# One step per chunk, crossbar transposes on the ACT queue and an earlier start of the weights, in a kernel that runs retention attention into an MLP

## The chip, the cores and the metric

The kernel runs on one core of one Trainium2 chip. The metric is the device time of one execution in microseconds (us). An execution more than 1.5% above the fastest of its kernel is counted as slow. "Median" is over four executions unless stated. A ratio is the mean time of one kernel's fast runs over that of the other's fast runs of the same rounds, so it is not quite the ratio of the medians quoted beside it; the brackets after it are a 95% interval. "Faster" or "slower" is given only where the difference is clearly over 2%.

Engine names: PE is the matrix engine, DVE the vector engine, ACT the scalar engine, POOL the general engine, SP the engine that here only starts transfers. "ACTq" and "SPq" in a timeline are DMA issues: the time an engine's instruction stream spends on starting a transfer.

## The reference

```python
# q, k, v: batch 8, heads 8, sequence 576, head size 64
scores = scale * q @ k.transpose
ret    = scores * D          # D[i, j] = gamma_h ** (i - j) for i >= j, else 0
x      = (ret @ v), heads side by side -> 4608 tokens x 512
h      = x @ w_in            # 512 -> 2048
g      = h * cos(h)
out    = g @ w_out           # 2048 -> 512
```

## The kernel before

Retention is computed in chunks of 128 tokens, five per batch entry, 40 in all (the fifth has 64 tokens). For each chunk PE does four things:

- scores: keys against queries, 64-row operands (row tiling), into PSUM `sc`; DVE masks it with a triangle into `pt`;
- state: keys against values, accumulated in PSUM `st`; DVE turns it into `sbd`, in which only each head's own block may be nonzero;
- inter: state of the chunk before times the queries;
- intra: `pt` times the values, 64-column outputs (column tiling); DVE multiplies inter + intra by the decay `up` and writes `xt`, the MLP's input.

The MLP then has units. An mlp1 unit is four matmuls into one PSUM bank, a sine on ACT (`cb`; the cosine is a sine with a shifted argument) and a product on DVE (`gt`), which frees the bank. An mlp2 unit is four matmuls; four units fill a bank that ACT copies to `os`. Chunks and units are interleaved in program order, and each engine works through its own instructions in that order.

Keys and queries are needed transposed. For the first seven chunks PE does it (`step_tk`, `step_tq`); later it is a crossbar DMA, issued from SP, which also issues the input loads and the output stores.

```python
def move_k(self, g):
    self.P.add("sp", lambda e: e.dma_start_transpose(KT[t] <- NAT[k]), ...)   # shortened
def move_q(self, d):
    self.P.add("sp", lambda e: e.dma_start_transpose(QT[t] <- QNAT[k]), ...)  # shortened
# ...
def step_st(self, g):
    def mm(e):
        for c in range(4):
            inst = e.matmul(
                ap(self.ST, 512, 0, 128, c * 128, [1, 128]),
                ap(self.NAT[k], 2 * DM, 0, n, c * 128, [1, 128]),
                ap(self.NAT[k], 2 * DM, 0, n, DM + c * 128, [1, 128]),
                start=(r == 0 and c == 0), stop=True, skip_group_check=True)
        return inst
    self.P.add("pe", mm, ...)
    self.P.add("dve", ... SBD = ST * BDM ...)     # 128x512 product with a block mask
# ...
BYPE, LEAD = 7, 2
def T(g):
    load_to(g + LEAD + 4)                # SP: loads
    cast_to(g + LEAD + 2)                # POOL: casts to bf16
    if g < BYPE:                         # PE transposes
        if pair(g):
            self.step_tq(dbl(g))
        self.step_tk(g)
    x = g + LEAD
    if BYPE <= x < NC:                   # crossbar transposes
        if pair(x):
            self.move_q(dbl(x))
        self.move_k(x)
# ...
def run(mlp, att):                       # spreads the attention steps over the mlp units
    n, m, k = len(att), len(mlp), 0
    for i, u in enumerate(mlp):
        u()
        while k < n * (i + 1) // m:
            att[k]()
            k += 1

def att_of(g0, g1):
    for g in range(g0, g1):
        out += [T(g + 1), ST(g), step_o(g), S_(g + 1)]    # as lambdas
```

The schedule has three stages. Stage 1 is the start-up and the first mlp1 pass. Stage 2 runs from the first mlp2 matmul to the first 512-wide mlp1 matmul after it; it holds the second block of mlp1 units (320 and 192 tokens wide) and about ten chunks. Stage 3 is the steady state, blocks of 512 tokens: 32 mlp units and about four chunks each, then a tail without chunks.

Of the kernel before, what the change touches and what calls it, by code (L numbers as in the profile page):

```python
# [101 lines left out]
class Kernel:  # L102
    def __init__(self, nc, es, q, k, v, w_in, w_out, out):
        self.nc = nc
        self.P = Prog(nc, es)
        self.src = [q.tensor, k.tensor, v.tensor]
        self.w_in, self.w_out, self.out = w_in.tensor, w_out.tensor, out.tensor
        sb = nc.alloc_sbuf_tensor
        self.NSTG, self.NNAT, self.NKT, self.NQ, self.NQT = 7, 6, 5, 3, 4
        self.NPT, self.NSB, self.NCB, self.NOS = 2, 2, 3, 3  # L110
        self.XT = sb("xt", [128, 4 * TOK], BF16)
        self.WIN = sb("win", [128, 4 * DFF], BF16)
        self.WOUT = sb("wout", [128, NF * DM], BF16)
        self.STG = [sb(f"stg{i}", [128, 2 * DM], F32) for i in range(self.NSTG)]
        self.NAT = [sb(f"nat{i}", [128, 2 * DM], BF16) for i in range(self.NNAT)]
        self.KT = [sb(f"kt{i}", [128, DM], BF16) for i in range(self.NKT)]
        self.QSTG = [sb(f"qstg{i}", [128, 2 * DM], F32) for i in range(self.NQ)]
        self.QNAT = [sb(f"qnat{i}", [128, 2 * DM], BF16) for i in range(self.NQ)]
        self.QT = [sb(f"qt{i}", [128, 2 * DM], BF16) for i in range(self.NQT)]
        self.PT = [sb(f"pt{i}", [128, 1024], BF16) for i in range(self.NPT)]  # L120
        self.SBD = [sb(f"sbd{i}", [128, 512], BF16) for i in range(self.NSB)]
        self.GT = [sb(f"gt{i}", [128, NF * TB], BF16) for i in range(2)]
        self.CB = [sb(f"cb{i}", [128, TB], BF16) for i in range(self.NCB)]
        self.OS = [sb(f"os{i}", [128, DM], F32) for i in range(self.NOS)]
        self.UP = sb("up", [128, 4 * S], F32)
        self.WV = sb("wv", [128, 40], F32)
        self.IDN = sb("idn", [128, 128], BF16)
        self.TRI = sb("tri", [128, 128], BF16)
        self.BDM = sb("bdm", [128, 128], BF16)
        self.ONE = sb("one", [128, 128], BF16)  # L130
        self.DUM = sb("dum", [128, 512], BF16)
        self.IG = sb("ig", [128, S], F32)
        self.IV = sb("iv", [128, 40], F32)
        self.LV = sb("lv", [128, 40], F32)
        self.LU = sb("lu", [128, 4], F32)
        self.CLN = sb("cln", [128, 1], F32)
        self.CPI = sb("cpi", [128, 1], F32)
        self.SC = nc.alloc_psum_tensor("sc", [128, 1024], F32)
        self.ST = nc.alloc_psum_tensor("st", [128, 512], F32)
        self.BK = [nc.alloc_psum_tensor(f"bk{i}", [128, 512], F32) for i in range(5)]  # L140
        self.held, self.turn = {0}, 0
        self.n_cb = self.n_os = 0
# [10 lines left out]
    def constants(self):  # L153
# [4 lines left out]
        P.add("pool", lambda e: e.iota(ap(self.IG, S, 0, 128, 512, [1, 64]), [[1, 2], [2, 32]], base=512,  # L158
                                       channel_multiplier=0, allow_small_or_imprecise_dtypes=True), w=["ig"])
# [3 lines left out]
        P.add("dve", lambda e: e.memset(self.DUM.ap(), 0.0), w=["dum"])  # L163
        for h in range(H):
            P.add("dve", lambda e, h=h: e.memset(ap(self.LV, 40, 0, 128, h, [8, 5]), -lng[h]), w=[("lv", h)])  # L165
            P.add("dve", lambda e, h=h: e.memset(ap(self.LU, 4, 64 * (h % 2), 64, h // 2, [1, 1]), lng[h]),
                  w=[("lu", h)])
        P.add("dve", lambda e: e.memset(self.CLN.ap(), math.log(1.0 / 8.0)), w=["cln"])
        P.add("dve", lambda e: e.memset(self.CPI.ap(), math.pi / 2), w=["cpi"])
        P.add("dve", lambda e: e.memset(self.BDM.ap(), 0.0), w=["bdm"])  # L170
        P.add("dve", lambda e: e.memset(ap(self.BDM, 128, 0, 64, 0, [1, 64]), 1.0), w=["bdm"])
        P.add("dve", lambda e: e.memset(ap(self.BDM, 128, 64, 64, 64, [1, 64]), 1.0), w=["bdm"])
        P.add("dve", lambda e: e.tensor_tensor(self.LV.ap(), self.IV.ap(), self.LV.ap(), ALU.mult),
              r=["iv"] + [("lv", h) for h in range(H)], w=["lvx"])
        P.add("act", lambda e: e.activation(self.WV.ap(), self.LV.ap(), AF.Exp), r=["lvx"], w=["wv"])
        for c in range(4):
            P.add("act", lambda e, c=c: e.activation(
                ap(self.UP, 4 * S, 0, 128, c * S, [1, S]), self.IG.ap(), AF.Exp,
                bias=self.CLN.ap(), scale=ap(self.LU, 4, 0, 128, c, [1, 1])),
                r=["ig0", "ig", "cln", ("lu", 2 * c), ("lu", 2 * c + 1)], w=["up"])  # L180
# [5 lines left out]
                                                channel_multiplier=-1), r=["one"], w=["tri"])  # L186

# [17 lines left out]
    def load_win(self, s, gate=()):  # L205
        self.P.add("pool", lambda e: e.dma_start(  # L206
            ap(self.WIN, 4 * DFF, 0, 128, s * 512, [DFF, 4], [1, 512]),
            bass.AP(self.w_in, s * 512, [[DFF, 128], [128 * DFF, 4], [1, 512]])),
            r=list(gate), w=[("win", s)], sem=f"wi{s}")
# [78 lines left out]
    def move_k(self, g):  # L288
        n, k, t = CHUNKS[g][2], g % self.NNAT, g % self.NKT
        self.P.add("sp", lambda e: e.dma_start_transpose(  # L290
# [3 lines left out]
    def move_q(self, d):  # L294
        n, k, t = (128, 128, 32)[d % 3], d % self.NQ, d % self.NQT
        self.P.add("sp", lambda e: e.dma_start_transpose(
# [11 lines left out]
    def step_s(self, g):  # L308
        n = CHUNKS[g][2]
        kt, pt, h = self.KT[g % self.NKT], self.PT[g % self.NPT], n // 2  # L310
# [10 lines left out]
        self.P.add("pe", mm, r=[("kt", g % self.NKT), self.qkey(g)], w=["sc"])  # L321
        self.P.add("dve", lambda e: e.tensor_tensor(  # L322
# [5 lines left out]
    def step_st(self, g):  # L328
        b, r, n = CHUNKS[g]
        k = g % self.NNAT  # L330

        def mm(e):
            for c in range(4):
                inst = e.matmul(  # L334
                    ap(self.ST, 512, 0, 128, c * 128, [1, 128]),
                    ap(self.NAT[k], 2 * DM, 0, n, c * 128, [1, 128]),
                    ap(self.NAT[k], 2 * DM, 0, n, DM + c * 128, [1, 128]),
                    start=(r == 0 and c == 0), stop=True, skip_group_check=True)
            return inst

        self.P.add("pe", mm, r=[("nat", k, 0), ("nat", k, 1)], w=["st"])
        self.P.add("dve", lambda e: e.tensor_tensor(  # L342
            ap(self.SBD[g % self.NSB], 512, 0, 128, 0, [128, 4], [1, 128]),
            ap(self.ST, 512, 0, 128, 0, [128, 4], [1, 128]),
            ap(self.BDM, 128, 0, 128, 0, [0, 4], [1, 128]), ALU.mult),
            r=["st", "bdm"], w=[("sbd", g % self.NSB)])

    def step_o(self, g):
        b, r, n = CHUNKS[g]
        na, pt, h = self.NAT[g % self.NNAT], self.PT[g % self.NPT], n // 2  # L350
        sbd = self.SBD[(g - 1) % self.NSB]
        i, ob, key = self.bank()

        def inter(e):
# [6 lines left out]
        def intra(e):  # L361
# [9 lines left out]
        if r:  # L371
            self.P.add("pe", inter, r=[("sbd", (g - 1) % self.NSB), self.qkey(g)], w=[key])
        self.P.add("pe", intra, r=[("nat", g % self.NNAT, 1), ("pt", g % self.NPT)], w=[key])
# [4 lines left out]
            r=[key, "up"], w=[("xt", g)])  # L378


    def mlp1(self, lo, hi, f):
# [17 lines left out]
        self.P.add("pe", mm, r=[("win", f // 4)] + xts, w=[key])  # L399
# [38 lines left out]
    def schedule(self):  # L438
# [4 lines left out]
        BYPE, LEAD = 7, 2  # L443
# [27 lines left out]
        def T(g):  # L471
            if g >= NC:
                return
            load_to(g + LEAD + 4)
            cast_to(g + LEAD + 2)
# [9 lines left out]

        def ST(g):
            if CHUNKS[g][1] < 4:
                self.step_st(g)

        def S_(g):  # L490
            if g < NC:
                self.step_s(g)
# [9 lines left out]
        def att_of(g0, g1):  # L502
            out = []
            for g in range(g0, g1):
                out += [lambda g=g: T(g + 1), lambda g=g: ST(g), lambda g=g: self.step_o(g), lambda g=g: S_(g + 1)]
# [14 lines left out]

        load_to(4)
        warm(10)
        for g in range(4):
            self.cast_k(g, "act")
            if g % 2 == 0:
                self.cast_q(g // 2, ("act", "dve"))
            self.cast_v(g, "pool")
            if g == 2:
                self.load_win(0, [("stg", 3, 0)])
                self.load_win(1)  # L530
            self.step_tk(g)
            if g % 2 == 0:
                self.step_tq(g // 2, "dve")
            if g:
                self.step_o(g - 1)
            self.step_s(g)
            self.step_st(g)
            if g < 3:
                warm(2)
        self.load_win(2)  # L540
        self.load_win(3)
# [4 lines left out]
        cast_to(6)  # L546
        self.mlp1(0, 256, 0)
        self.step_o(3)
        for f in (1, 2, 3):
            self.mlp1(0, 256, f)  # L550
# [6 lines left out]
        att = [lambda: T(4), lambda: S_(4)] + att_of(4, 7)  # L557
# [53 lines left out]
```

## Time and profile before

The median was 342.63 us (341.87 to 343.41, four runs).

| | start of stage 2 | start of stage 3 | span | stage 2 | stage 3 |
|---|---|---|---|---|---|
| before, profiled run, us | 35.9 | 96.1 | 339.4 | 60.2 | 243.3 |

From the page of the kernel before: the engines' busy times with share of the span and number of instructions, then three groups of instructions (line, engine, operation, output and inputs, shape, count; busy us, mean ns; idle us ahead of them and what ended most of it).

```profile
PE 311.9 (92%) x2184; PEld 158.8 (47%) x2220; DVE 189.8 (56%) x304; ACT 139.7 (41%) x223; POOL 96.3 (28%) x137
...
L393 PE MATMUL bk<-xt,win 128*128 128x512 bf16 (+3 forms) x640 | 147.5, 360 | 3.0 <-issue 1.3
...
L315 PE MATMUL sc<-qt,kt 64*128 64x128 bf16 (+1 forms) x320 | 16.1, 223 | 11.8 <-DMA kt<-nat 10.6
...
L334 PE MATMUL st<-nat 128*128 128x128 bf16 x128 | 13.5, 233 | 0.0
```

PE is the bottleneck on average. The one large idle term is scores (L315) waiting for transposed keys. ACT is busy 41% of the span. The PE timeline of the kernel before shows where the keys are late (start us, length us, what; in brackets the idle time before it and what ended it):

```profile
64.47 0.61 PE L315 MATMUL sc<-qt,kt 64*128 64x128 bf16 x8 [6.54 <-DMA kt<-nat]
```

Three more such waits, of 1.55, 1.88 and 0.66 us, follow by 96 us. The SP timeline of the same kernel shows what the keys stood behind:

```profile
58.96 2.89 SPq L296 DMA_TRANSPOSE qt<-qnat  x1
61.90 1.26 SPq L290 DMA_TRANSPOSE kt<-nat  x1
63.20 0.58 SPq L433 DMA_DIRECT2D out_dram<-os  x1
63.83 0.42 SPq L192 DMA_DIRECT2D stg<-in_k_dram  x1
```

The key transpose is issued only at 61.90, behind a query transpose that held SP for 2.89 us. In stage 3 there is no such wait, and the timeline of PE shows the shape of the work instead:

```profile
120.08 0.39 PE L356 MATMUL bk<-qt,sbd 128*128 128x128 bf16 x4
120.40 0.41 PE L364 MATMUL bk<-pt,nat 128*64 128x128 bf16 x8
120.75 1.04 PE L393 MATMUL bk<-xt,win 128*128 128x512 bf16 x4
121.62 1.03 PE L415 MATMUL bk<-wout,gt 128*128 128x512 bf16 x4
122.58 0.40 PE L315 MATMUL sc<-qt,kt 64*128 64x128 bf16 x8
```

Read the starts, not the lengths, because matmuls overlap: inter to intra is 0.32 us, intra to the next unit 0.35, and an mlp unit takes 0.87 from start to start. The state stands alone further up (119.00, and the next unit at 119.22). The four parts of a chunk sit in three places, with mlp units between them. The tiling mode of PE ("128*128", "64*128", "128*64") changes at intra and back, and at scores and back.

One block of 512 tokens took (262.42 - 129.84) / 4 = 33.1 us, from one block's first mlp1 to the same place four blocks on.

### The profile page before, as it was taken

What the parts mean: (1) busy time and instruction counts of PE and PEld (TensorE: products, weight loads), DVE (VectorE), ACT (ScalarE), POOL (GpSimd) and SP (SyncE); (2) the same over time, 40 slices, a digit from 0 to 9 for tenths busy, and PEclk for the clock granted to TensorE, in tenths of its full rate; (3) what the DMA queues carried; (4) which work ended last, traced back from release to release, by engine and by line L of the source; (5) the groups of instructions that cost most, each with busy time, mean ns of one, the idle gap of its engine ahead of it and who ended that gap; (6) DMA issues with size and microseconds to landing.
All of it is one profiled execution on the core that took longest, in us unless ns stands there. A gap on an engine that the chain in (4) does not pass through costs nothing.

```text
span 339.4 us, 5764 instructions
## 1 busy us (share of the span) xinstructions
PE 311.9 (92%) x2184; PEld 158.8 (47%) x2220; DVE 189.8 (56%) x304; ACT 139.7 (41%) x223; POOL 96.3 (28%) x137
## 2 busy tenths in 40 slices
PE   5799888498799999999999999999999999999997
PEld 2564344266554444444444444444444444444444
DVE  2697315288765766566665766566756565433300
ACT  7457332156333333334434334433343334444411
POOL 3460265545445443140424333322320000000000
PEclk9589999589899999999999999999999999999999
DMA  9999999999999997676669963847861101100012
GB/s 186 184 187 201 194 254 229 208 238 174 212 192 178 230 228 168 156 155 163 148 113 246 186 140 97 201 108 172 194 87 47 47 31 38 56 33 32 31 62 95
DMA packets 135307, 50.06 MB, mean 147 GB/s; under 512 B 108016, under 2 KB 130800, under 8 KB 135280
## 3 DMA queue, kind: packets, MB, share of 16 engines
q1 hardware_dynamic: 131056, 45.50, 63.9%
q0 software_dynamic: 4224, 4.19, 7.7%
q8 instruction: 18, 0.29, 0.4%
q14 instruction: 9, 0.07, 0.1%
HBM read 36.70 MB, written 9.44 MB: 136 GB/s over the span
## 4 chain that ended last, share of the span: by engine, by line
PE 70%; DMA 14%; SPq 6%; POOL 3%; issue 2%; DVE 2%; ACT 1%; DVEq 0%; POOLq 0%
PE bk L415 33%; PE bk L393 30%; DMA wout<-in_moe_w_out_dram 5%; DMA qstg<-in_q_dram 5%; DMA kt<-nat 4%; SPq L192 3%; PE sc L315 2%; PE bk L364 2%; DMA stg<-in_k_dram 2%; PE st L334 1%; PE bk L356 1%; POOL win L206 1%; DVE gt L403 1%; SPq L290 1%; SPq L200 1%
## 5 line engine op out<-in xcount | busy, mean ns | idle before, releaser
L400 ACT ACTIVATE cb<-bk,cpi 128x512 bf16<-128x512 f32 (+3 forms) x164 | 103.8, 635 | 151.3 <-PE bk L393 150.3
L403 DVE TENSOR_TENSOR gt<-bk,cb 128x512 bf16<-128x512 f32 (+3 forms) x164 | 101.8, 625 | 100.0 <-ACT cb L400 97.5
L393 PE MATMUL bk<-xt,win 128*128 128x512 bf16 (+3 forms) x640 | 147.5, 360 | 3.0 <-issue 1.3
L415 PE MATMUL bk<-wout,gt 128*128 128x512 bf16 (+1 forms) x573 | 142.1, 373 | 3.4 <-DMA wout<-in_moe_w_out_dram 1.3
L415 PEld LDWEIGHTS bk<-wout,gt 128*128 128x128 bf16 x592 | 55.3, 98 | 65.0 <-ACT os L430 3.7
L393 PEld LDWEIGHTS bk<-xt,win 128*128 128x128 bf16 x656 | 59.4, 100 | 54.7 <-DVE xt L374 2.1
L322 DVE TENSOR_TENSOR pt<-sc,tri 128x1024 bf16<-128x1024 f32 (+1 forms) x40 | 44.3, 1106 | 17.4 <-PE sc L315 17.4
L222 POOL CAST nat<-stg 128x512 bf16<-128x512 f32 (+1 forms) x36 | 21.9, 609 | 110.5 <-DMA stg<-in_k_dram 93.0
L232 POOL TENSOR_TENSOR nat<-stg,wv 128x512 bf16<-128x512 f32 (+1 forms) x40 | 41.7, 1043 | 24.2 <-DMA stg<-in_v_dram 15.1
L430 ACT ACTIVATE os<-bk 128x512 f32<-128x512 f32 (+1 forms) x37 | 21.7, 586 | 29.9 <-PE bk L415 29.9
L374 DVE TENSOR_TENSOR xt<-bk,up 128x512 bf16<-128x512 f32 (+1 forms) x40 | 26.7, 668 | 6.8 <-PE bk L364 6.7
L222 POOL CAST qnat<-qstg 128x512 bf16<-128x512 f32 (+1 forms) x44 | 25.8, 612 | 16.4 <-DMA qstg<-in_q_dram 15.4
L315 PE MATMUL sc<-qt,kt 64*128 64x128 bf16 (+1 forms) x320 | 16.1, 223 | 11.8 <-DMA kt<-nat 10.6
L342 DVE TENSOR_TENSOR sbd<-st,bdm 128x512 bf16<-128x512 f32 x32 | 21.8, 680 | 1.0 <-PE st L334 1.0
L315 PEld LDWEIGHTS sc<-qt,kt 64*128 64x128 bf16 (+1 forms) x320 | 9.3, 100 | 26.4 <-issue 12.7
L364 PE MATMUL bk<-pt,nat 128*64 128x128 bf16 (+1 forms) x320 | 16.2, 224 | 0.4 <-DVE pt L322 0.4
L334 PE MATMUL st<-nat 128*128 128x128 bf16 x128 | 13.5, 233 | 0.0
L334 PEld LDWEIGHTS st<-nat 128*128 128x128 bf16 x128 | 10.2, 104 | 6.4 <-issue 0.4
L356 PEld LDWEIGHTS bk<-qt,sbd 128*128 128x128 bf16 x128 | 9.7, 103 | 7.2 <-ACT cb L400 0.8
L364 PEld LDWEIGHTS bk<-pt,nat 128*64 128x64 bf16 (+1 forms) x320 | 10.0, 111 | 6.5 <-issue 2.5
L356 PE MATMUL bk<-qt,sbd 128*128 128x128 bf16 (+1 forms) x128 | 12.2, 221 | 0.6 <-DVE gt L403 0.6
L517 PE MATMUL bk<-dum,one 128*128 128x512 bf16 x15 | 6.8, 603 | 1.6 <-DVE lv L165 1.4
(36 smaller groups left out, 39.8 us busy)
## 6 DMA issues: line engine op xcount, KB each, us to landing
out_dram<-os SPq DMA_DIRECT2D x35, 256.0 KB, 2.2
stg<-in_k_dram SPq DMA_DIRECT2D x32, 256.0 KB, 3.6
qstg<-in_q_dram SPq DMA_DIRECT2D x16, 512.0 KB, 5.2
stg<-in_v_dram SPq DMA_DIRECT2D x32, 256.0 KB, 5.2
win<-in_moe_w_in_dram POOLq DMA_DIRECT2D x4, 512.0 KB, 8.3
wout<-in_moe_w_out_dram POOLq DMA_DIRECT2D x4, 512.0 KB, 14.9
stg<-in_k_dram SPq DMA_DIRECT2D x8, 128.0 KB, 3.3
qstg<-in_q_dram SPq DMA_DIRECT2D x8, 128.0 KB, 3.2
```

The costliest lines, as they stand in the source:

```text
L222: self.P.add(eng, lambda e: e.tensor_copy(dst, src), r=r, w=w)
L232: self.P.add(eng, lambda e: e.tensor_tensor(ap(self.NAT[na], 2 * DM, 0, n, DM, [D, H], [1, D]), ap(self.STG[st], 2 * DM, 0, n, DM, [D, H], ...
L315: inst = e.matmul(ap(self.SC, 1024, 0, n, hp * 512 + c * 128, [1, n]), ap(kt, DM, 64 * hp, 64, c * 128, [1, n]), self.queries(g, 64 * hp, ...
L322: self.P.add("dve", lambda e: e.tensor_tensor(ap(pt, 1024, 0, n, 0, [128, 8], [h, 2], [1, h]), ap(self.SC, 1024, 0, n, 0, [128, 8], [h, 2] ...
L334: inst = e.matmul(ap(self.ST, 512, 0, 128, c * 128, [1, 128]), ap(self.NAT[k], 2 * DM, 0, n, c * 128, [1, 128]), ap(self.NAT[k], 2 * DM, 0 ...
L356: inst = e.matmul(ap(ob, 512, 0, 128, c * 128, [1, n]), ap(sbd, 512, 0, 128, c * 128, [1, 128]), self.queries(g, 0, 128, c), start=(c == 0 ...
L364: inst = e.matmul(ap(ob, 512, 64 * hp, 64, c * 128, [1, n]), ap(na, 2 * DM, 0, n, DM + (2 * c + hp) * D, [1, D]), ap(pt, 1024, 0, n, hp * ...
L374: self.P.add("dve", lambda e: e.tensor_tensor(ap(self.XT, 4 * TOK, 0, 128, b * S + CH * r, [TOK, 4], [1, 2], [2, h]), ap(ob, 512, 0, 128, ...
L393: inst = e.matmul(ap(ps, 512, 0, 128, 0, [1, n]), ap(self.WIN, 4 * DFF, 0, 128, c * DFF + 128 * f, [1, 128]), ap(self.XT, 4 * TOK, 0, 128, ...
L400: self.P.add("act", lambda e: e.activation(ap(cb, TB, 0, 128, 0, [1, n]), ap(ps, 512, 0, 128, 0, [1, n]), AF.Sin, bias=self.CPI.ap(), scal ...
L403: self.P.add("dve", lambda e: e.tensor_tensor(ap(gt, NF * TB, 0, 128, f * TB + lo - TB * j, [1, n]), ap(ps, 512, 0, 128, 0, [1, n]), ap(cb ...
L415: return e.matmul(ap(ps, 512, 0, 128, 0, [1, cn]), ap(gt, NF * TB, 0, 128, f * TB + 128 * t, [1, 128]), ap(self.WOUT, NF * DM, 0, 128, f * ...
```

## The change

The intent has three parts.

1. One step per chunk: inter, state, intra and the next chunk's scores stand together, in an order with fewer changes of tiling mode. The state is computed only for each head's own 64 columns, so no mask is needed; two DVE copies of 64x256 replace the masked 128x512 product.
2. Crossbar transposes are issued from ACT instead of SP, and ahead of the loads in `T`; PE transposes now serve ten chunks instead of seven. The aim is that keys no longer wait behind loads and stores.
3. The start-up is reordered: w_in is issued sooner and its first pieces are smaller, the decay is computed in two parts.

```diff
 def move_k(self, g):
-    self.P.add("sp", lambda e: e.dma_start_transpose(
+    self.P.add("act", lambda e: e.dma_start_transpose(
 # ... and the same in move_q

+def mm_st(self, g):              # the state, 64 columns of one head at a time
     for c in range(4):
-        inst = e.matmul(ap(self.ST, 512, 0, 128, c * 128, [1, 128]), ...)
+        for hp in range(2):
+            inst = e.matmul(
+                ap(self.ST, 512, 64 * hp, 64, c * 64, [1, 64]),
+                ap(self.NAT[k], 2 * DM, 0, n, (2 * c + hp) * D, [1, D]),
+                ap(self.NAT[k], 2 * DM, 0, n, DM + (2 * c + hp) * D, [1, D]), ...)
+def ev_st(self, g):
-    # one DVE product 128x512 with the block mask
+    for hp in range(2):
+        self.P.add("dve", lambda e, hp=hp: e.tensor_copy(
+            ap(self.SBD[g % self.NSB], 512, 64 * hp, 64, 64 * hp, [128, 4], [1, 64]),
+            ap(self.ST, 512, 64 * hp, 64, 0, [64, 4], [1, 64])), ...)

+def step(self, g):
+    i, ob, key = self.bank()
+    self.mm_inter(g, ob, key)
+    self.mm_st(g)
+    self.mm_intra(g, ob, key)
+    self.mm_s(g + 1)             # the next chunk's scores
+    self.ev_o(g, ob, key)        # DVE: xt
+    self.ev_st(g)                # DVE: sbd, two copies
+    self.ev_s(g + 1)             # DVE: pt

-BYPE, LEAD = 7, 2
+BYPE, LEAD = 10, 2
 def T(g):
-    load_to(g + LEAD + 4)
-    cast_to(g + LEAD + 2)
     # ... the transposes ...
+    load_to(g + LEAD + 4)
+    cast_to(g + LEAD + 2)

-    out += [T(g + 1), ST(g), step_o(g), S_(g + 1)]
+    out += [T(g + 1), step(g)]

 # start-up, cut to what the argument touches
+    self.step_tk(1)
+    self.decay(256, S, "ig0", "ig1")     # second part of the decay, four Exp on ACT
+    self.sin_table()                     # makes ACT load the sine's table here
     # ...
+    self.load_win(0, 1, [("stg", 2, 0)]) # w_in one chunk sooner, in five loads for four, the first two half as large
     # ...
     self.cast_k(2, "act")
```

## The prediction

> **What bounds the kernel now.** Three stages, by the page's slices, the windows and the PE timeline.
> 1. 0 to 36 us: start-up, then the first mlp1 pass. The clock is 0.55 from 10 to 20 us; PE nearly gapless from 22.45 us.
> 2. 36 to 96 us: PE should do about 40 us of work (27.6 us of mlp, nine chunks, transposes) and takes 60. The PE timeline has gaps of 1.3, 1.3, 6.5, 1.6, 0.6, 1.9 and 0.7 us, the large ones ended by "DMA kt<-nat"; half clock follows two of them (about 4.5 us more). DMA moves 203 to 237 GB/s. The transposes sit on SP behind loads and stores; chunk 11's k load is issued at 63.8 us, behind two of them.
> 3. 96 to 323 us: PE-bound, 98% busy. One block of 512 tokens takes 33.1 us; its 32 mlp units are 27.65 us (0.864 each), so a chunk costs 1.25 us.
>
> **The change in stage 3.** Start to start, the timeline gives: state 0.22 us, inter 0.32, intra 0.35, scores 0.33 plus about 0.10 ahead of them. Streaming alone is about 0.21 each; the rest is switching. The Trainium skill (TensorEngine Tiling, Key Properties) says that changing the tiling mode drains the array, and this trace agrees, with about 0.1 us per change. One step per chunk (inter, state, intra, scores) has three changes for four and a state of half the columns: my estimate is 1.05 us for 1.25. 27 chunks: 5 us saved. DVE now gets 2.6 us in one burst after a step; the banks should cover it. A block's last step now stands just before the mlp1 that needs it: 0.2 us worse per block.
>
> **Crossbar transposes on ACT.** 30 kt and 18 qt issues, 1.25 us and 1.3 us (SP timeline, late, when unloaded; 2 to 3.7 us loaded), are about 61 us of ACT time (41% busy before). A pair blocks sin for about 2.6 us; banks allow about 3.5. Mostly hidden. The skill (DMA: Bandwidth & Descriptors, Issuing engines are not separate DMA queues) grants no bandwidth; the gain is order: loads no longer stand behind transposes, nor these behind stores.
>
> **Stage 2.** Chunks 7 to 9 now go through PE transposes, so the 6.5 us gap should vanish. But the first moved transpose (q10, ahead of the next sin) makes ACT wait for data that lands about 26 us after the weights: new PE gaps of 2 to 4 us there, and once or twice later. Estimate: stage 2 ends at 86 to 88 us instead of 96: 8 us saved.
>
> **Stage 1.** Weights start about 2.5 us sooner (the DMA gap at 15 to 18 us closes), removing the 1.3 us wait for wout. Scores 0 come 1.5 us sooner, but decay's second part and the sin table now precede chunk 2 on ACT. About zero on PE.
>
> **Sum:** 342.8 - 8 - 5 + 1 = 331 us, range 323 to 340. Chances: faster 0.74, same 0.19, slower 0.07.
>
> **Right if:** PE gaps at 57 to 96 us shrink from 11 to about 6 us; a block takes about 32.2 us; the state group falls from 13.5 to about 7 us busy; waits for kt nearly vanish; ACT waits on POOL casts appear near 57 us.
>
> **Wrong if:** transpose issues on ACT take 3 us each under load, sin comes late and PE waits for banks (DVE gt) throughout stage 3, eating the gain; or DMA, not order, limits stage 2 (chunk 15 no sooner than 89 us); or the half clock returns after a new gap.

## The result and the profile after

The median went up to 347.27 us (346.19 to 347.97, four runs), a ratio of 1.0132 [1.0097, 1.0168]: clear of noise, though under 2%. All outputs are right. The prediction was 331, with a range of 323 to 340: wrong in direction and outside the range.

| profiled run, us | start of stage 2 | start of stage 3 | span | stage 2 | stage 3 |
|---|---|---|---|---|---|
| before | 35.9 | 96.1 | 339.4 | 60.2 | 243.3 |
| after | 38.6 | 98.5 | 346.2 | 60.0 | 247.7 |
| difference | +2.6 | | +6.8 | -0.2 | +4.4 |
| predicted difference | 0 | | -12 | -8 | -4 |

(The spans are of one profiled run each; their difference of 6.8 us is larger than the 4.6 us between the medians, within the scatter of single runs.)

Against the prediction the shortfall is in every stage; against the kernel before, stages 1 and 3 are longer and stage 2 is as long as it was. From the page after: busy times, and the groups that answer to those shown of before.

```profile
PE 307.4 (89%) x2337; PEld 158.8 (46%) x2374; DVE 194.1 (56%) x335; ACT 141.6 (41%) x233; POOL 96.2 (28%) x138
...
L444 PE MATMUL bk<-xt,win 128*128 128x512 bf16 (+3 forms) x634 | 147.3, 363 | 21.0 <-DVE gt L454 8.0
...
L320 PE MATMUL sc<-qt,kt 64*128 64x128 bf16 (+1 forms) x320 | 15.9, 222 | 1.4 <-DVE qt L228 1.2
...
L346 PE MATMUL st<-nat 128*64 128x64 bf16 x256 | 10.4, 205 | 0.2 <-POOL nat L238 0.2
```

PE is busy 4.5 us less than before, which fits a cheaper step. The waits for keys are gone (11.8 us of idle ahead of scores became 1.4). But mlp1 (L444) now has 21.0 us of idle time ahead of it, where it had 3.0. ACT still reads "41%", because the issues it now makes are not counted. In the list of PE's waits (what waited, for what; total us, times, longest us) the kernel before had these:

```profile
PE sc L315 <- DMA kt<-nat: 10.6, 4, 6.5
PE bk L393 <- DVE xt L374: 1.3, 3, 0.6
PE bk L415 <- ACT os L430: 0.7, 1, 0.7
```

The list after names new ones:

```profile
PE bk L444 <- DVE gt L454: 8.0, 5, 2.6
PE bk L444 <- DVE xt L399: 7.5, 8, 1.8
PE bk L466 <- ACT os L481: 4.2, 4, 1.6
PE bk L266 <- ACT nat L226: 3.5, 2, 2.8
```

All four end in ACT or run through it, but not all of this is the transposes' doing: e1 below, without them on ACT, keeps part of it. **Stage 2**, the ACT timeline after, where keys of chunk 9 and the first moved transposes come:

```profile
61.96 0.59 ACT L226 ACTIVATE kt<-bk 128x512 bf16<-128x512 bf16 x1
63.21 1.33 ACTq L302 DMA_TRANSPOSE qt<-qnat  x1
64.57 1.69 ACTq L296 DMA_TRANSPOSE kt<-nat  x1
66.30 1.37 ACT L451 ACTIVATE cb<-bk,cpi 128x320 bf16<-128x320 f32 x3 [3.76 <-POOL nat L228]
```

The PE timeline after, just behind it:

```profile
67.57 1.25 PE L444 MATMUL bk<-xt,win 128*128 128x320 bf16 x8 [2.57 <-DVE gt L454]
```

The sine at 66.30 is said to have waited 3.76 us for POOL. Read the lines above it before believing that: ACT finished a copy at 62.55, waited 0.66 us for its data, and then spent 1.33 + 1.69 = 3.02 us on issuing two transposes. The few hundredths left are between the instructions. Then came the sine, then the product `gt` (66.93 in DVE's timeline), and only then did a PSUM bank come free for PE, which had stood still for 2.57 us.

**Stage 3**, the chain of waits after, around the place where a block of tokens ends (start us, length us, what):

```profile
130.33 0.69 ACT cb L451
131.02 0.56 ACTq L302
131.59 0.03 issue
131.62 1.69 ACTq L296
133.30 0.05 issue
133.35 0.70 ACT cb L451
...
134.14 0.69 DVE gt L454
134.83 0.64 DVE xt L399
135.47 0.27 issue
135.75 0.81 PE bk L444 x3
```

And the PE timeline of the same place:

```profile
132.72 0.39 PE L372 MATMUL bk<-qt,sbd 128*128 128x128 bf16 x4
133.04 0.32 PE L346 MATMUL st<-nat 128*64 128x64 bf16 x8
133.19 0.39 PE L387 MATMUL bk<-pt,nat 128*64 128x128 bf16 x8
133.51 0.40 PE L320 MATMUL sc<-qt,kt 64*128 64x128 bf16 x8
135.75 0.81 PE L444 MATMUL bk<-xt,win 128*128 128x512 bf16 x3 [1.84 <-DVE xt L399]
```

PE had finished intra by about 133.6, but `xt` started only at 134.75 in DVE's timeline (the chain counts it from the end of `gt`, 134.83). DVE works in order, and `gt` stood before `xt` in its stream; `gt` waited for the sine, and the sine for the two issues. The next block's first mlp1 needs this `xt`, and nothing is left between them to hide it. The waits for `os` arise on ACT alone, as its timeline and PE's show ten microseconds earlier:

```profile
122.28 1.19 ACTq L302 DMA_TRANSPOSE qt<-qnat  x1
123.51 1.27 ACTq L296 DMA_TRANSPOSE kt<-nat  x1
124.89 0.60 ACT L481 ACTIVATE os<-bk 128x512 f32<-128x512 f32 x1 [1.92 <-PE bk L444]
125.54 1.04 PE L466 MATMUL bk<-wout,gt 128*128 128x512 bf16 x4 [1.57 <-ACT os L481]
```

The copy to `os` stood behind the same two issues, and the next mlp2 unit behind the copy; the other long wait for `os`, 1.65 us at 260.76, looks the same.

**Stage 1**, the ACT timeline after:

```profile
10.12 2.28 ACT L185 ACTIVATE up<-ig,cln,lu 128x320 f32<-128x320 f32 x4
12.42 1.28 ACT L191 ACT_TABLE_LOAD   x1
13.82 0.61 ACT L226 ACTIVATE nat<-stg 128x512 bf16<-128x512 f32 x1
```

The keys of chunk 2 are cast at 13.82 (12.56 before), behind the second part of the decay and the table load. PE waited 2.80 us for that cast; before, PE waited for such a cast only once, 1.9 us, for chunk 0.

### The profile page after: what moved, and what is told of

Its sections match the earlier page's. It is cut to its first block, busy times and chain, and to the rows that moved or that the text cites. A ratio compares the mean times of both kernels' runs of the same rounds, so it can differ in the third digit from the quotient of the medians.

```text
span 346.2 us, 6065 instructions
## 1 busy us (share of the span) xinstructions
PE 307.4 (89%) x2337; PEld 158.8 (46%) x2374; DVE 194.1 (56%) x335; ACT 141.6 (41%) x233; POOL 96.2 (28%) x138
## 3 DMA queue, kind: packets, MB, share of 16 engines
q10 hardware_dynamic: 29184, 7.08, 13.1%
## 4 chain that ended last, share of the span: by engine, by line
PE 70%; ACT 6%; issue 6%; DVE 4%; POOL 4%; ACTq 3%; DMA 3%; SPq 3%; DVEq 0%; POOLq 0%
PE bk L444 33%; PE bk L466 29%; ACT cb L451 3%; ACTq L296 3%; SPq L198 2%; PE sc L320 2%; POOL nat L238 2%; DVE gt L454 2%; PE st L346 2%; DMA stg<-in_v_dram 2%; PE bk L387 2%; POOL qnat L228 2%; DVE xt L399 1%; PE bk L372 1%; DMA qstg<-in_q_dram 1%
## 5 line engine op out<-in xcount | busy, mean ns | idle before, releaser
L451 ACT ACTIVATE cb<-bk,cpi 128x512 bf16<-128x512 f32 (+3 forms) x164 | 102.6, 635 | 159.4 <-PE bk L444 119.7
L444 PE MATMUL bk<-xt,win 128*128 128x512 bf16 (+3 forms) x634 | 147.3, 363 | 21.0 <-DVE gt L454 8.0
L454 DVE TENSOR_TENSOR gt<-bk,cb 128x512 bf16<-128x512 f32 (+3 forms) x164 | 100.7, 624 | 108.8 <-ACT cb L451 87.0
L444 PEld LDWEIGHTS bk<-xt,win 128*128 128x128 bf16 x656 | 62.5, 101 | 80.7 <-DVE xt L399 9.4
L466 PEld LDWEIGHTS bk<-wout,gt 128*128 128x128 bf16 x592 | 56.1, 98 | 71.0 <-ACT os L481 9.0
L399 DVE TENSOR_TENSOR xt<-bk,up 128x512 bf16<-128x512 f32 (+1 forms) x40 | 26.7, 669 | 11.8 <-PE bk L387 10.9
L359 DVE CAST sbd<-st 64x256 bf16<-64x256 f32 x64 | 26.5, 414 | 1.0
L387 PEld LDWEIGHTS bk<-pt,nat 128*64 128x64 bf16 (+1 forms) x320 | 10.4, 114 | 1.6 <-DVE pt L331 1.1
L346 PE MATMUL st<-nat 128*64 128x64 bf16 x256 | 10.4, 205 | 0.2 <-POOL nat L238 0.2
L346 PEld LDWEIGHTS st<-nat 128*64 128x64 bf16 x256 | 6.8, 114 | 5.9 <-issue 3.5
L226 ACT ACTIVATE kt<-bk 128x512 bf16<-128x512 bf16 (+1 forms) x10 | 5.5, 550 | 4.6 <-PE bk L266 4.6
```

Source lines behind the costliest of these rows:

```text
L359: self.P.add("dve", lambda e, hp=hp: e.tensor_copy(ap(self.SBD[g % self.NSB], 512, 64 * hp, 64, 64 * hp, [128, 4], [1, 64]), ap(self.ST, 5 ...
L387: inst = e.matmul(ap(ob, 512, 64 * hp, 64, c * 128, [1, n]), ap(na, 2 * DM, 0, n, DM + (2 * c + hp) * D, [1, D]), ap(pt, 1024, 0, n, hp * ...
L399: self.P.add("dve", lambda e: e.tensor_tensor(ap(self.XT, 4 * TOK, 0, 128, b * S + CH * r, [TOK, 4], [1, 2], [2, h]), ap(ob, 512, 0, 128, ...
L444: inst = e.matmul(ap(ps, 512, 0, 128, 0, [1, n]), ap(self.WIN, 4 * DFF, 0, 128, c * DFF + 128 * f, [1, 128]), ap(self.XT, 4 * TOK, 0, 128, ...
L451: self.P.add("act", lambda e: e.activation(ap(cb, TB, 0, 128, 0, [1, n]), ap(ps, 512, 0, 128, 0, [1, n]), AF.Sin, bias=self.CPI.ap(), scal ...
L454: self.P.add("dve", lambda e: e.tensor_tensor(ap(gt, NF * TB, 0, 128, f * TB + lo - TB * j, [1, n]), ap(ps, 512, 0, 128, 0, [1, n]), ap(cb ...
```

## The experiments

The theory after reading the traces: the transposes cost the gain, through the 1.2 to 2.3 us during which each holds ACT's in-order stream; sine, `gt`, `xt` and `os` come late. Rivals: (a) the step itself, by its position just before the block that needs it, or by its burst of work on DVE; (b) the start-up's order on ACT; (c) data, not issue: ACT waits for the POOL casts that the transposes read, or the transfers themselves are slow; (d) ten PE-transposed chunks instead of seven. The first four runs shared one chip and one set of runs of the kernel before (median 342.32); then four (341.99), four (342.63) and two (342.26). Each of these groups ran on a chip of its own.

For stages 2 and 3 I made the same sums for each version: the listed waits of PE in the timeline, and the time lost to a halved clock, which is the length of a stretch times (1 - mean granted clock) from the windows view. The second counts idle time too, so it is a little high. All in us.

| version | stage 2 | PE waits | half clock | rest | stage 3 | PE waits | half clock | rest |
|---|---|---|---|---|---|---|---|---|
| before | 60.2 | 14.5 | 6.6 | 39.1 | 243.3 | 2.0 | 0 | 241.3 |
| after | 60.0 | 13.1 | 7.2 | 39.7 | 247.7 | 10.3 | 1.2 | 236.2 |
| e1 after, transposes on SP | 52.4 | 7.8 | 3.7 | 40.9 | 240.7 | 5.0 | 0 | 235.7 |
| e6 after, last step earlier | 56.9 | 12.1 | 4.0 | 40.8 | 239.7 | 0.7 | 2.7 | 236.3 |
| e5 e1, last step earlier | 51.0 | 8.3 | 1.5 | 41.2 | 237.0 | 0.7 | 0 | 236.3 |
| e8 e5, ACT order at start | 50.9 | 9.4 | 0 | 41.5 | 237.0 | 0.7 | 0 | 236.3 |
| e9 e1, seven PE chunks | 52.0 | 9.3 | 3.6 | 39.1 | 240.9 | 4.0 | 0 | 236.9 |
| e13 e9, loads first | 55.4 | 11.5 | 5.0 | 38.9 | 240.9 | 4.0 | 0 | 236.9 |

(Stage 2 waits include the one that ends where stage 3 starts. Stage 3 waits are summed from 100 us on, without gaps of 0.16 us that are put down to "issue": they come where a matmul's record is missing. The clock column of stage 3 is the half clock that still lasts at its beginning.) The "rest" columns hardly move. Stage 3 has about 236 us of work with the new step and 241 with the old one, whatever the queue; stage 2 has about 41 with ten chunks transposed on PE (after: 39.7) and 39 with seven. Nearly everything else is waits and the clock. Each row is one trace. After and e6 run the same program up to stage 3, and their stages 2 differ by 3.1 us (60.0 and 56.9), most of it the clock; e1 and e5, alike in the same way, differ by 1.4. So a difference of up to about 3 us in stage 2 between two rows proves nothing by itself.

### e1: the change, with the transposes back on SP

```diff
 # after; in move_k and move_q
-self.P.add("act", lambda e: e.dma_start_transpose(
+self.P.add("sp", lambda e: e.dma_start_transpose(
```

> The changed kernel with its crossbar transposes issued from SP again, in the same program order; nothing else differs. Theory A (the issues on ACT hold sin, os and then DVE behind them): the PE waits for xt at the block boundaries fall from about 0.96 us each to the 0.4 of before, the waits for os vanish, stage 3 shortens by 8 to 10 us, and the kernel takes 334 to 339 us. Rival B (the one-step order itself: its DVE burst and its place as the last unit of a block): the boundary waits stay at 0.7 us or more, and the time stays within 2 us of 347.

Measured: 333.15 us, ratio 0.974 [0.969, 0.979]. The queue of the transposes alone is worth 347.27 - 333.15 = 14.1 us; the two were run in different rounds, and by their ratios to their own before it is (1.0132 - 0.974) x 342.6 = 13.4 us. Stage 2 fell to 52.4, stage 3 to 240.7. Theory A is right about the time, but not in each of its numbers: stage 3 fell by 7.0 us and not by 8 to 10, stage 2 gave the rest, and the boundary waits stayed at 0.50 to 0.77 us, about what rival B said of them. The place in stage 3 that answers to the one shown of after, in the DVE timeline of this version:

```profile
124.33 0.69 DVE L454 TENSOR_TENSOR gt<-bk,cb 128x512 bf16<-128x512 f32 x1 [1.04 <-ACT cb L451]
125.11 0.73 DVE L399 TENSOR_TENSOR xt<-bk,up 128x512 bf16<-128x512 f32 x1
```

and in the PE timeline:

```profile
126.11 0.81 PE L444 MATMUL bk<-xt,win 128*128 128x512 bf16 x3 [0.72 <-DVE xt L399]
```

`gt` is on time: `xt` starts 0.91 us after inter (124.20 in PE's timeline) instead of 2.03 (132.72 to 134.75), and the mlp1 at 126.11 waits 0.72 us instead of 1.84. What remains, 0.72 us, is not the issues'; e5 shows that it belongs to the step's position.

Rival (c) can be read from the traces. In the ACT timeline of after, ACT stood idle ahead of only one of its 48 transposes, for 0.66 us (the one at 63.21 above); all others were issued while the instruction before them still ran or right behind it. So waiting for the casts cost ACT almost nothing, and the holes in its work are the issues. From issue to landing a key transpose took 3.9 us on the ACT queue and 3.2 on SP's (queries 5.2 and 4.5), so the transfer was slower from ACT, if anything, but PE waits for no crossbar keys in either. The mean issue time was 1.39 us for 30 key and 1.25 us for 18 query transposes on ACT, 64 us in total.

### e2: the kernel before, with the transposes on ACT

```diff
 # before; in move_k and move_q
-self.P.add("sp", lambda e: e.dma_start_transpose(
+self.P.add("act", lambda e: e.dma_start_transpose(
```

> The kernel before with only the issuing engine of the transposes changed, SP to ACT. Theory A: stage 3 gets longer by 6 to 10 us through late sin and os, time 348 to 354 us. Rival B: the position of the step is needed for the harm; stage 3 stays within 2 us of 217 us and the time within 3 us of 343.

Measured: 349.98 us, ratio 1.0228 [1.0164, 1.0292], so 7.7 us slower than before's 342.32. The move costs time without the rest of the change as well, so it is not an interaction with the new step alone. Its interval reaches across 2%. Stage 2 took 65.3 us for before's 60.2. In its list of waits stand 10.1 us for `gt` and 6.6 for `os` where before had 10.6 for keys and 0.7 for `os`: the wait was exchanged, not removed. The profiled run also had a stretch at 186 to 195 us with a mean clock of 0.62, which is worth 9 x 0.38 = 3.4 us of its stage 3 of 250.5; I do not use that stage's length. (The 217 us of the expectation is not stage 3 as defined here, which took 243.3 us before.)

### e3: the kernel before, with the new step alone

```diff
 # before, with after's mm_*, ev_* and step
-out += [T(g + 1), ST(g), step_o(g), S_(g + 1)]
+out += [T(g + 1), step(g)]
```

> The kernel before with only the one-step order and the 64-column state; transposes stay on SP, start-up and the seven chunks of PE transposes as before. Theory A: stage 3 shortens by 4 to 5 us, time 337 to 339 us. Rival B: boundary waits grow to about 1 us each and DVE bursts hold banks; time 343 us or more.

Measured: 341.37 us, ratio 0.997 [0.9931, 1.0009]: no difference that the runs resolve, and between the two expectations. In the stages, stage 3 gained 2.6 us (240.7 for 243.3) and stage 2 lost 1.7. The step does not cause the slowdown, but it also does not give its 5 us.

### e4: the kernel before, with the new start alone

```diff
 # before, with after's constants, decay, sin_table, load_win and start-up sequence
```

> The kernel before with only the start-up of the changed kernel: decay in two parts, sin table early, weights sooner and in finer pieces, other order of chunks 0 to 3. If the start-up is what lost time there: mlp2 begins 2.6 us later (38.5 instead of 35.9 us) and the time is 1 to 3 us longer, 344 to 346 us. If only the transposes did it: within 1 us of 343.

Measured: 340.07 us, ratio 0.9929 [0.9868, 0.9991]. Stage 2 started 2.1 us later (38.0) and was 2.6 us shorter; the weights' wait of 1.3 us is gone. The time met neither branch of the expectation: on balance the start is a small gain (the interval ends just under 1), so rival (b) is not what made the change slower. It could still be better than it is, which e7 tries.

### e5 and e6: the last step of a block earlier

In stage 3 the steps of a block are spread over all its 32 mlp units, so the last one stands right before the mlp1 that needs it. Here they are spread over the first 28. e5 is e1 with this edit; e6 is the changed kernel with it, transposes on ACT.

```diff
-def run(mlp, att):
-    n, m, k = len(att), len(mlp), 0
+def run(mlp, att, spare=0):
+    n, m, k = len(att), len(mlp) - spare, 0
     for i, u in enumerate(mlp):
         u()
-        while k < n * (i + 1) // m:
+        while k < min(n, n * (i + 1) // m):
 # the calls of stage 3:
-    run(mlp, att_of(need[j + 1], need[j + 2]) if j + 2 < NTB else [])
+    run(mlp, att_of(need[j + 1], need[j + 2]) if j + 2 < NTB else [], 4)
```

> The changed kernel with its transposes on SP, and the steps of a block spread over 28 of its 32 mlp units, so that the last step ends four units before the mlp1 that reads its xt. If the position of the last step costs what is left at the boundaries: the waits for xt, 6.2 us in all, fall to about 1 (those of stage 2 stay), and stage 3 falls from 240.7 to 236 to 237 us. If the waits come from the DVE burst wherever it stands: they move to gt or os, and stage 3 stays at 239 us or more.

> The changed kernel with its transposes still on ACT, and the steps spread over 28 of 32 units. If the ACT issues do their harm in stage 3 mainly through the boundary (late sin, late gt, late xt): stage 3 falls from 247.7 us to about 241. If they do it everywhere (os and banks), it stays at 244 us or more.

Measured: e5 329.10 us, ratio 0.9624 [0.9585, 0.9663]; e6 338.14 us, ratio 0.9893 [0.9851, 0.9934]. This pair decides stage 3. On SP the edit gained 3.7 us there (240.7 to 237.0), on ACT 8.0 (247.7 to 239.7). In e6 the PE timeline from 100 us on has no wait for `xt` at all and 0.7 us for `os`, where after had 5.8 and 4.5 us. With four units of slack, the same issues on ACT do no visible harm in stage 3: e6's stage is 2.6 us longer than e5's, and its first 14.2 us ran at a mean clock of 0.81 (e5: 1.00), which is 2.7 us carried over from stage 2. So in stage 3 the transposes on ACT hurt only with the steps spread to the block's end. For `xt` the reason is the missing slack; that the waits for `os` vanish too is measured, but not taken apart: the edit also moves the issues relative to the copies to `os`. In stage 2, e6 keeps most of the loss: 56.9 against 51.0.

### e7 and e8: the order on ACT at the start

e7 is e1 with the second part of the decay and the table load moved behind the casts of chunks 2 and 3; e8 is e5 with the same.

```diff
     self.step_tk(1)
-    self.decay(256, S, "ig0", "ig1")
-    self.sin_table()
     self.step_o(0)
     # ...
     self.cast_k(3, "act")
+    self.decay(256, S, "ig0", "ig1")
+    self.sin_table()
     self.cast_v(3, "pool")
```

> The changed kernel with its transposes on SP, and on ACT the second decay part and the sin table moved from before the casts of chunk 2 to after the cast of chunk 3's k. If that place delays the start: the 2.7 us PE wait for the cast of chunk 2's k vanishes, mlp2 begins 2 to 4 us sooner than the 38.5 to 40.6 us of the two runs that have it, and the time falls from 333 to 330 or 331 us, unless the data of chunk 4 then ends the wait. If not: within 1 us of 333.

> Both edits on top of the changed kernel with its transposes on SP. If the two gains add, since they lie in different stages: 326 to 329 us.

Measured: e7 330.67 us, ratio 0.969 [0.9644, 0.9735]; e8 327.06 us, ratio 0.9568 [0.9531, 0.9604]. Chunk 2 is cast at 10.59 us instead of 13.82, and PE's wait of 2.8 us for it is gone; part of it comes back as a wait for the cast of the next queries (2.4 us in e7, 1.5 in e1). Against e1 (another chip's rounds) e7's median is 2.5 us lower; against e5, of the same rounds, e8's is 2.0 us lower. Part of this is the clock: both ran stage 2 without any half clock, where e1 lost 3.7 us to it. The start of stage 2 is not a clean measure: after, e1 and e5 have the same start-up (no crossbar transpose is issued before 63 us in after), and reached stage 2 at 38.6, 40.6 and 38.4. From 20 to 30 us, after and e5 had a mean clock of 0.88 and 0.87, e1 0.71. The Trainium skill (TensorE: Matmul & The Clock Gate, What's actually happening) says that the activity window is free-running, so that one kernel's count of slow matmuls varies with its phase at the start. These three traces fit that, with 2.2 us between them; no run here isolates it.

### e9 and e13: seven chunks on PE, and the order of loads and transposes on SP

e9 is e1 with seven PE-transposed chunks as before; e13 is e9 with loads and casts ahead of the transposes again.

```diff
 # e9
-BYPE, LEAD = 10, 2
+BYPE, LEAD = 7, 2
 # e13, in T, in addition
+load_to(g + LEAD + 4)
+cast_to(g + LEAD + 2)
 # ... transposes ...
-load_to(g + LEAD + 4)
-cast_to(g + LEAD + 2)
```

> The changed kernel with its transposes on SP and chunks 7 to 9 back on the crossbar (seven chunks of PE transposes for ten). If the ten chunks are what closes the 6.5 us gap of stage 2: a PE wait of 6 us or more for kt comes back near 60 us, stage 2 falls back from 52.4 to 58 us or more, the time is 338 to 341 us. If the order of issue (transposes ahead of loads) closes it: no such wait, 333 us plus or minus 1.5.

> The changed kernel with transposes on SP, seven chunks of PE transposes, and, on SP and POOL, the loads and casts of later chunks ahead of the transposes again, as the kernel before had it. If the order transposes ahead of loads is what saved stage 2 (the previous run kept its 52 us without the three extra chunks): stage 2 goes back to 57 us or more with kt waits of 8 us or more, the time to 338 us or more. If neither the order nor the number of chunks matters by itself, and the sooner weights do it: stage 2 stays below 55 us.

Measured: e9 336.01 us, ratio 0.9798 [0.9732, 0.9864]; e13 338.36 us, ratio 0.9863 [0.9794, 0.9931]. With seven chunks the waits for keys come back (5.2 us in three waits in e9, 6.5 in two in e13), but stage 2 keeps its length (52.0 against 52.4), because waits for `gt` shrink and PE has fewer transposes to do (the rest falls from 40.9 to 39.1). Neither branch of e9's expectation was met. Ten against seven is therefore not settled: the medians of e1 and e9 differ by 2.9 us, across jobs, and the intervals of their ratios overlap. Issuing the transposes ahead of the loads on SP is worth about 3.4 us of stage 2 in the traces (55.4 against 52.0) and 2.4 us in the medians, again with overlapping intervals; 3.4 us is hardly more than the 3.1 by which two traces of one program differed. If it is real, it is the effect that the move to ACT was meant to have, and it was to be had on SP.

### e10 and e11: the order and the 64-column state apart

e10 is the kernel before in the one-step order, but with the 128-column state and the masked product. e11 is the kernel before in its old order, but with the 64-column state and the two copies.

```diff
 # e10: before with step(), mm_st as before (128 columns, BDM)
-out += [T(g + 1), ST(g), step_o(g), S_(g + 1)]
+out += [T(g + 1), step(g)]
 # e11: before with after's mm_st and ev_st, the old att_of
```

> The kernel before with the one-step order but the full 128-column state and its masked product. If a change of tile shape costs PE about 0.1 us: the state group stays 0.22 us long plus a change, one change per chunk is saved, 27 chunks give 2.7 us, and the later xt at six boundaries takes about 2.6 back, so stage 3 is 243 us plus or minus 0.7 and the time 342 to 344. If the order alone were the whole gain: stage 3 240.7 us as with both.

> The kernel before with the state in 64-column tiles but in the old order, the state alone between two mlp units. If a change of tile shape drains the array for 0.1 us: the state now has a change on each side that it had not, which is worth more than its halved columns, so stage 3 grows by 1 to 3 us, to 244.5 or 246 us. If halving the columns is a gain by itself: stage 3 falls by about 2.5 us.

Measured: e10 342.92 us, ratio 1.0004 [0.9957, 1.0051], stage 3 0.3 us shorter than before's: by the same sums the order saved 2.2 us of work there, and the late last step took 1.9 back in waits for `xt`. e11 344.99 us, ratio 1.0062 [1.002, 1.0104], stage 3 2.9 us longer. Together (e3) they were 2.6 us shorter, and with the last step early (e5) 6.3. Why the narrow state alone is worse is seen in the PE timeline of e11:

```profile
112.26 1.03 PE L459 MATMUL bk<-wout,gt 128*128 128x512 bf16 x4
113.22 0.32 PE L339 MATMUL st<-nat 128*64 128x64 bf16 x8
113.46 1.04 PE L437 MATMUL bk<-xt,win 128*128 128x512 bf16 x4
```

Between two mlp units it takes from 113.12 (112.26 + 0.86) to 113.46, 0.34 us, of which 0.10 is ahead of it; the 128-column state took 0.22, with the same tiling as its neighbours. The Trainium skill (TensorEngine Tiling (Array Packing), Key Properties) says that a change of tiling mode drains the array. The 0.10 us ahead of it and the 2.9 us of stage 3 fit that: the narrow tile pays only where it stands next to intra, which has the same mode. In the one step, state to intra is 0.15 us (133.04 to 133.19 above).

### e12 and e15: one of the two state copies on ACT

e8 with one copy of each pair on ACT, everywhere (e12) or in `step()` only (e15), to shorten DVE's burst after a step (`xt` 0.7, copies 0.86, `pt` 1.1 to 1.2 us).

```diff
 def step(self, g):
-    self.ev_st(g)                      # both copies on DVE
+    self.ev_st(g, ("dve", "act"))      # the second on ACT
```

> The fastest so far (transposes on SP, last step early, decay later on ACT), with one of the two copies of the state moved from DVE to ACT, so that DVE's burst after a step is 0.43 us shorter. If the burst is what holds banks in stage 2 (6.4 us of waits for gt): those fall to 4 or 5 us and the time to 325 or 326 us. If ACT is as tight there: 327 us or more.

> The fastest kernel so far with one of the two state copies on ACT in the steps only, not in the start-up, where the copy on ACT had made chunk 1's k wait. If the shorter DVE burst is worth the 3 us that stage 2 fell by (50.9 to 47.7 us), and the start-up is the 37.1 us of the kernel without it: 323 to 325 us. If the late start was chance (the clock) and stage 2 only took back what it lost: 326 to 328 us.

Measured: e12 327.67 us, ratio 0.9565 [0.952, 0.961]; e15 327.44 us (324.11 to 329.35), ratio 0.9523 [0.9454, 0.9592]. One of e15's four runs, 329.35, was slow; the median of the three fast ones is 326.86. In the traces stage 2 fell from 50.9 to 47.7 and 48.0 us, with waits for `gt` down from 6.4 to 4.1. The medians did not follow (e8: 327.06). In e12 one reason shows: its stage 2 began at 40.8 us instead of e8's 37.1, with PE waiting for casts and keys that ACT makes; e15 began at 37.0. So the traces show less waiting for `gt` in stage 2, but the runs do not show that a shorter burst shortens the kernel; that stays open. It is in any case not the cause of the slowdown, since e8 has the full burst.

e8, e12 and e15 cannot be told apart and are the best versions: about 327 us, 4.3 to 4.8% faster than before and 20 us faster than the change as given.

## Why the prediction was wrong

**The step that failed** is "A pair blocks sin for about 2.6 us; banks allow about 3.5. Mostly hidden." The size was right: the prediction said 61 us of ACT time in issues, and 64 was measured; a pair held ACT for 3.0 us in the stretch shown. What was wrong is what this reaches.

- In stage 2 the allowance was taken from stage 3. Four banks at 0.86 us per unit give 3.5 us, but the units there are 320 or 192 tokens wide and take 0.53 or 0.32 us, and all of them are mlp1. By the same estimate four banks last 2.1 or 1.3 us. Waits for `gt` (8.0 us) and `cb` (2.3) took the place of the waits for keys (10.6 us), and the half clock stayed (7.2 us for 6.6), once right after a new gap, as "Wrong if" had said. PE's gaps at 57 to 96 us, which were to shrink from 11 to about 6 us, came to 11.8. Not all of that is the issues': without them e1 still waits 4.8 us for `gt` and 0.5 for `cb`. So the predicted 8 us was gained (e1: 7.8) and taken back whole, by 5.3 us more of waits (13.1 for 7.8) and 3.5 us more of half clock; the clock's part varies by about as much between traces of one program (e6 lost 4.0).
- In stage 3 the banks did hold: there is no wait for `gt` there, which "Wrong if" had named. The delay went by two other ways that the prediction did not look at: through DVE's order to `xt`, and through ACT's own order to `os`. After e1 is subtracted they cost 5.3 us of stage 3 (10.3 less 5.0; 1.8 for `xt` and 3.5 for `os`), and the carried half clock 1.2, of 7.0 lost.

**"0.2 us worse per block"** was mis-sized. In e1, without the ACT issues, most block boundaries show waits of 0.5 to 0.8 us for `xt`, and moving the last step away gained 3.7 us. With the issues on ACT it was 8.0 us. The reason in the trace is a serial chain without an mlp unit left to cover it: intra, then `xt` at 0.7 us, then mlp1.

**"About zero on PE" in stage 1** failed at the place the prediction itself named: the decay's second part and the sine's table "now precede chunk 2 on ACT". PE waited 2.80 us for chunk 2. Stage 2 began 2.6 us later than before, with up to 2 us of scatter from the clock. The weights part was right: the 1.3 us wait for w_out is gone.

**The gain of the step** was right: 5 us predicted, 241.3 - 236.3 = 5.0 us of stage 3's work in the table above (before against e5), 6.3 us in length once the last step is early. But "a block takes about 32.2 us" came out as (301.28 - 135.75) / 5 = 33.1, as before, because the waits gave it back. The state group was to fall to 7 us busy and fell to 10.4: halving the columns doubled the matmuls (128 to 256), at 205 ns for 233.

**The order gain in stage 2** was right in part and wrong about its price. The waits for keys went from 10.6 us to 0, but that took the ten PE chunks too: without them (e9) 5.2 us of waits remain, though the stage is as short. "ACT waits on POOL casts" appear (6.0 us in two waits), but in the one taken apart above 3.0 of 3.76 us are the issues themselves, and its other 0.66 us is all the idle time that ACT spent ahead of an issue.

**The sign.** Of the predicted 11.8 us, e1 gained 9.2 (342.32 to 333.15). The one term that turned it was the transposes' queue: 13 to 14 us, booked as "mostly hidden".

**The skill.** The prediction leaned on the Trainium skill (DMA: Bandwidth & Descriptors, Issuing engines are not separate DMA queues): a second issuing engine saves only the time it takes to initiate the DMA, "which is usually small relative to the DMA itself". Bandwidth was indeed not gained: 225 GB/s in stage 2 with the transposes on ACT and 225 with them on SP. But 1.25 to 1.39 us of issue beside 3.9 to 5.2 us from issue to landing is not small, and on a compute engine it stops the work that stands behind it, as the two stretches above show. The same page (Silent corruption: two transposing streams in flight at once) says that transposes issued from two engines at once can corrupt each other, so keys on SP with queries on ACT, without waits between them, was not a way out; no run tried it.

What stays open: why the waits for `os` go in e6; the value of DVE's shorter burst in stage 2 (e12, e15); ten or seven PE chunks; and how far the half clock, rather than the waits that bring it on, separates single versions in stages 1 and 2.

## What to carry to other kernels

A DMA issue is work for the engine that makes it, though the busy share does not show it: before moving issues to a "41% busy" engine, lay each one into that engine's order and follow what stands behind it, to every consumer and not only to the bank. Take the slack for that from the stage in question, because by the same sum four banks last 3.5 us in one stage and 1.3 in another. And when parts of a step are fused, leave some independent work between the last of them and its consumer: here four units of slack were worth 3.7 us, and 8.0 with a late producer.

## What the Trainium skill lacked or had wrong

- DMA: Bandwidth & Descriptors, Issuing engines are not separate DMA queues: "usually small relative to the DMA itself" misleads for crossbar transposes within SBUF. Their issue took 1.39 us (keys) and 1.25 us (queries) on ACT on average, up to 2.29, and on SP 1.46 and 1.72 in e1, up to 2.9, with landing after 3 to 5 us. For this chip by name that page gives no issue time of a transpose (it has cycle counts of unnamed "previous generations", beside those of another chip), and it does not warn that an in-order compute engine pays it: here 13 to 14 us of 347.
- TensorEngine Tiling (Array Packing), Key Properties: the drain is named without a size. About 0.1 us per change here; a 64-column state alone between 128-column neighbours cost 0.34 us where the 128-column one cost 0.22 (e11: stage 3 longer by 2.9 us).
- TensorE: Matmul & The Clock Gate, HAM oscillation — how this bites in real kernels: the section shows it with DMA waits of about 3 to 5 us that cross a window of 3.4 us, and the section after it names short idles between groups of matmuls that cycle through PSUM banks, without their length. Here shorter waits, for another engine, stood before it, and their length alone did not decide: after a wait of 1.63 us for `gt` at the same place of stage 2, twelve 320-wide matmuls took 3.36 us in e1 and 1.79 us in e8. In the changed kernel they took 3.36 us after 2.13 us, and the half clock cost up to 7.2 us of the 60.0 us of stage 2. No run isolates what decides it.
